# A Fourier transform and an MLP on one core: the opening reordered, and x folded by accumulating DMA

## The chip, the core and the metric

One core of a Trainium2 chip. The metric is the device time of one execution, in microseconds (us). A core has TensorE (PE; its weight loads are shown apart as PEld), VectorE (DVE), ScalarE (ACT), GpSimd (POOL) and SyncE (SP, which here only issues DMAs). Each takes its instructions in the order of the program. 16 DMA engines move what SyncE, ScalarE and GpSimd issue.

## The reference

Batch 8, sequence 3136, width 256. First the real part of a two-dimensional Fourier transform of each batch entry, then a layer norm and an MLP with a residual:

```
X = fft(fft(x, axis=1), axis=2).real                    # x: 8 x 3136 x 256
mu, var = mean(X, -1), mean((X - mu)**2, -1)
Xn = (X - mu) / sqrt(var + 1e-6) * g_ln
out = X + maximum(Xn @ w1, 0) @ w2                      # w1: 256 x 1024, w2: 1024 x 256, both float64
```

## The kernel before, in words

*The transform over the sequence.* 3136 = 56 x 56, so the kernel does it in two steps. The host gathers x's rows so that the rows n and 3136-n of 28 residues stand together: `xs` holds, per tile `i` of 7, two rows n and two rows 3136-n for each of 112 partitions, and `xz` the lone residue. `fold_zw` adds the row n and the mirrored row 3136-n (mirrored along the width), into `z` and `w`; `ends` does that for the columns 0 and 128 into `e0c`; for batch 0 VectorE does `fold_zw`, for the other batches GpSimd. Step 1 (`step1`, `step1_ends`) is a matmul with `tu` over those sums, in batch 0 in plain float32; in the other batches sums and differences (`fold_eo`, GpSimd) are split into a rounded high part (`fold_hi`, ScalarE) and a low part (`fold_lo`, GpSimd) and multiplied in three passes. ScalarE copies step 1's result to `s1`, `store1` writes it to `scratch` in HBM, `relayout` reads it back with other partitions into `s2`, and step 2 (`step2`) is a matmul of `s2` with the table `tab_s`. Its result is stored in chunks of 256 tokens: full (`ck`), high (`ckh`) and low part (`ckl`).

*The MLP.* w1 is multiplied by `g_ln` and the transform over the width on the chip (`transform_w1(k, i)` adds half `i` of column block `k`; `round_w1(k)` makes the high part, `rest_w1(k)` and `rest_w1_copy(k)` the low part). A tile `s` is 128 hidden columns for one chunk; eight make a chunk. `moe1_a(s)` is six matmuls into `ab`, ScalarE's copy `asb` and VectorE's two combinations `h`; `moe1_b(s)` makes `h_hi` (ScalarE) and `h_lo` (VectorE); `moe2(s)` is twelve matmuls into `acc`, three passes with w2's high and low part. `residual`, `finish` and `store_out` end a chunk. The main loop is

```
for s in range(6, last):
    moe1_b(s - 1); moe1_a(s)
    # then late[s], moe2(s - 3), after[s]
```

where `after` and `late` are lists, written out by tile number, of everything else: step 1 and step 2 of the next batches, the loads of the batch after that, residuals and stores. There are 392 tiles.

*The weights.* w1 and w2 arrive as 64-bit floats in four quarters each. `convert_m`, `convert_b` (VectorE) and `convert_z` (ScalarE) pick mantissa, exponent and sign apart; `finish_w1`/`finish_w2` multiply them; `split_w2` makes w2's high (ScalarE) and low part (VectorE; GpSimd for the last quarter). w1's raw quarters lie in four buffers, `w1p`, and w2's quarters are loaded into the same four when these are free; quarter `n` of w2 serves the tiles 2n and 2n+1 of a chunk.

*The order ahead of the main loop* is written out by hand, for TensorE, VectorE, ScalarE, GpSimd and SyncE's DMA queue alike. Before: x of batch 0 and w1, then w2's quarters 0 and 1 as soon as w1's first two buffers are free, the first relayout (groups 0 to 3, in two parts, the second behind the last two stores of step 1), the tables, w2's quarters 2 and 3, x of batch 1. TensorE transforms all of w1, then five empty matmuls (`warm_up`), `step2(0)`, `step2(1)`, and the tiles 0 to 5, with the conversion of w2's quarters 2 and 3 beside them.

Lines of the profile: L212 and L210 load x, L596 w1, L601 w2; L226, L230 and L231 `ends`; L246 and L247 `fold_zw`, L257 and L258 `fold_eo`, L263 `fold_hi`, L269 `fold_lo`; L280 to L288 `step1_ends`; L299 and L300 step 1 of batch 0, L305 of the others, L309 its copy, L315 `store1`; L323 `relayout`; L355 and L359 `step2`, L376 `ckh`, L378 `ck`, L380 `ckl`; L400, L405 to L407 `moe1_a`, L414 and L415 `moe1_b`, L450 `moe2`; L567 to L582 the conversions, L586 and L587 `split_w2`, L610 `finish_w1`, L620 `transform_w1`, L628 `round_w1`, L633 `rest_w1`, L638 `rest_w1_copy`, L642 `finish_w2`, L722 `warm_up`.

Of the kernel before, what the change touches and what calls it, by code (L numbers as in the profile page):

```python
# [25 lines left out]
ALU = mybir.AluOpType  # L26
# [145 lines left out]
def tile_kernel(ctx: ExitStack, tc: tile.TileContext, x, x0, w1, w2, tu, tab, ty, tw, out):  # L172
# [27 lines left out]
    xs = const.tile([XP, NU, 4, D], F32, name="xs")  # L200
    xz = const.tile([XP, D], F32, name="xz")
# [5 lines left out]

    def load_x(b, i):
        if i == NU:
            in_order(nc.sync.dma_start(xz, x0[b]))  # L210
        else:
            in_order(nc.sync.dma_start(xs[:, i], x[b, i]))  # L212

    e0c, s1, scratch, s2, zw, pieces = {}, {}, {}, {}, {}, {}

    def ends(b, p0=0, p1=NS, eng=nc.gpsimd):

        if p0 == 0:
            e0c[b] = work.tile([XP, NS, 2], F32, tag="e0c", name=f"e0c{b}")
        e = e0c[b]  # L220
        i0, i1 = (p0 + 1) // 2, p1 // 2
        for j0, j1 in ((i0, min(i1, 6)), (max(i0, 6), i1)):
            if j0 < j1:
                xp = xs[:, j0:j1, :, 0:129:128]
                s0 = first_slot(j0)
                eng.tensor_tensor(out=e[:, s0:s0 + 2 * (j1 - j0)].rearrange("p (i a) c -> p i a c", a=2),  # L226
                                  in0=xp[:, :, 0:2], in1=xp[:, :, 2:4], op=ALU.add)
        if p1 < NS:
            return
        eng.tensor_copy(e[:, LONE], xz[:, 0:129:128])  # L230
        eng.tensor_tensor(out=masked.rearrange("p (c s) -> p c s", c=4),  # L231
                          in0=e[:, None, :, 0].to_broadcast([XP, 4, NS]),
                          in1=tu_s[:, 3 * XP:3 * XP + 4, None].to_broadcast([XP, 4, NS]), op=ALU.mult)

    def fold_zw(b, i, eng):

        if i == NU:
            return
        if i > 3 and b == 0:
            t = weights.tile([128, HW], F32, tag="h_hi", name=f"zw{b}_{i}", bufs=4)  # L240
        else:
            t = work.tile([128, 2 * 256], F32, tag="zw", name=f"zw{b}_{i}", bufs=3)
        z, w = (t[:, 256 * h:256 * h + 256].rearrange("p (s d) -> p s d", s=2) for h in range(2))
        zw[b, i] = z, w
        a, c = xs[:, i, 0:2], xs[:, i, 2:4]
        eng.tensor_tensor(out=z, in0=a[:, :, 1:129], in1=c[:, :, 255:127:-1], op=ALU.add)  # L246
        eng.tensor_tensor(out=w, in0=a[:, :, 255:127:-1], in1=c[:, :, 1:129], op=ALU.add)  # L247
# [28 lines left out]
    def step1_ends(b, p0=0, p1=NS):  # L276
# [3 lines left out]
        nc.tensor.matmul(ps[:, 0], tu_p, e0c[b][:, p0:p1, 1], start=True, stop=True)  # L280
        nc.tensor.matmul(ps[:, 1], tu_h, e0c[b][:, p0:p1, 0], start=False, stop=True,
# [8 lines left out]
    def step1(b, i):  # L290
# [4 lines left out]
        if b == 0:  # L295
            z, w = zw.pop((b, i)) if n > 1 else (xz[:, None, 1:129], xz[:, None, 255:127:-1])
# [253 lines left out]
    def convert_e(key, wp):  # L550
# [3 lines left out]
        else:  # L554
            e = work.tile([128, 512], F32, tag="zw", name=f"e{key}", bufs=3)
# [43 lines left out]
    def load_w2(n):  # L599
        wp = w1p[n]  # L600
# [25 lines left out]
    def round_w1(k):  # L626
        for j in range(2):
            nc.scalar.copy(w1_cols(w1_hi, k, j), psw[k, j])  # L628
# [47 lines left out]
    for b in range(1, NB):  # L676
# [4 lines left out]
        add(need - 62 if b > 1 else ends_at - 7, ends, b)  # L681
        add(ends_at, step1_ends, b)
        for i, d in sorted(enumerate(at), key=lambda p: p[1]):
            d0, d = d, d - (b == 1)
            add(d - 7, fold_zw, b, i, nc.gpsimd)
            if b + 1 < NB:
                add(d - 5, load_x, b + 1, i)
# [37 lines left out]
    with tc.manual_schedule(engines={E.PE, E.Activation, E.DVE, E.Pool}):  # L725
        with tc.manual_schedule(engines={E.SP}):
# [46 lines left out]
            ends(0, 10, NS)  # L773
# [3 lines left out]
            fold_zw(0, 5, nc.vector)  # L777
# [6 lines left out]
            fold_zw(0, 6, nc.vector)  # L784
# [4 lines left out]
            relayout(0, 0, 4, LONE - 2)  # L789
# [13 lines left out]
            convert_b("w1_3")  # L803
            load_w2(3)
# [100 lines left out]
```

## Time and profile before

| | |
|---|---|
| median of 3 runs | 989.62 us (989.11 to 989.96) |
| profiled execution | 991.33 us, its span 989.5 us, TensorE clock 1.00 |
| TensorE busy | 977.6 us of the span, 99% |
| VectorE, ScalarE, GpSimd busy | 811.8, 538.4, 259.8 us |
| DMA | 94.69 MB, 96 GB/s in the mean; 343 GB/s in the first 23 us |
| TensorE busy from 0 to 23, 23 to 31, 31 to 36, 36 to 70 us | 19.98, 7.54, 3.02, 31.39 us |
| TensorE busy from 970 to the end (19.5 us) | 15.68 us |

A row of the busy times by stretch gives the stretch, its length, then for each engine its busy time and its count of instructions, the granted clock of TensorE, the share of the 16 DMA engines and GB/s. A row of the timeline has the start, the duration, engine, line, operation, the tile written and those read; in brackets how long the engine was idle before and what ended that. A group has busy time and mean duration. A DMA's issue is short; "to landing" is from its issue to the last byte.

### The profile page before, as it was taken

The numbers are of one execution on the slowest core, as the hardware profiler recorded it, in microseconds if no ns is written. First come the engines' busy times: TensorE is split into PE (matmuls) and PEld (weight loads), VectorE is DVE, ScalarE is ACT, GpSimd is POOL, SyncE is SP. The second block draws the span as 40 slices with busy tenths as digits, with TensorE's granted clock in tenths as the row PEclk, the third lists the DMA queues.
The fourth block names the chain that finished last, engine by engine and source line by source line (L and its number), as shares of the span: only waits on it lengthen the run. The fifth ranks groups of instructions, "written<-read, shape, count | busy, mean of one in ns | idle before, by whom it ended". The sixth has DMA issues, their size and how long they took to land.

```text
span 989.5 us, 22022 instructions
## 1 busy us (share of the span) xinstructions
PE 977.6 (99%) x8386; PEld 963.2 (97%) x8386; DVE 811.8 (82%) x2185; ACT 538.4 (54%) x1415; POOL 259.8 (26%) x312
## 2 busy tenths in 40 slices
PE   8899999999999999999999999999999999999998
PEld 6689999999999999999999999999999999999998
DVE  6788887888788788878878887888788888888887
ACT  3556555555555555565555555555655554454553
POOL 2046622334123421442223332233213500000000
PEclk9999999999999999999999999999999999999999
DMA  9933342224122232222322241222210112100101
GB/s 349 337 115 111 118 168 71 86 92 149 55 91 75 92 131 84 70 97 75 145 81 76 87 150 69 79 89 91 107 44 34 65 38 108 39 27 23 44 23 44
DMA packets 43673, 94.69 MB, mean 96 GB/s; under 512 B 3952, under 2 KB 20592, under 8 KB 42672
## 3 DMA queue, kind: packets, MB, share of 16 engines
q1 hardware_dynamic: 42352, 91.18, 25.9%
q8 instruction: 67, 1.10, 0.5%
q0 software_dynamic: 400, 1.31, 0.3%
q10 hardware_dynamic: 816, 0.79, 0.2%
q14 instruction: 38, 0.31, 0.1%
HBM read 51.58 MB, written 41.68 MB: 94 GB/s over the span
## 4 chain that ended last, share of the span: by engine, by line
PE 92%; DVE 4%; DMA 2%; ACT 1%; issue 0%; SPq 0%; ACTq 0%
PE acc L450 51%; PE ab L400 26%; PE ps L355 5%; PE psy L475 4%; PE ps L305 4%; DVE h_lo L415 1%; DMA xs<-x 1%; DMA scratch<-s 1%; DVE h L406 1%; DVE h L407 1%; PE ps L299 1%; ACT h_hi L414 0%; PE ps L300 0%; DMA s<-scratch 0%; PE ps L359 0%
## 5 line engine op out<-in xcount | busy, mean ns | idle before, releaser
L450 PE MATMUL acc<-w_hi,h_lo 128*128 128x256 f32 x1568 | 433.6, 277 | 0.2 <-DVE h_lo L415 0.2
L450 PE MATMUL acc<-w_lo,h_hi 128*128 128x256 f32 x1568 | 433.3, 276 | 0.0
L450 PE MATMUL acc<-w_hi,h_hi 128*128 128x256 f32 x1568 | 433.3, 276 | 0.0
L415 DVE SCALAR_TENSOR_TENSOR h_lo<-h,h_hi 128x512 fp32r<-128x512 f32 x392 | 286.0, 729 | 146.2 <-ACT h_hi L414 140.9
L414 ACT ACTIVATE h_hi<-h 128x512 fp32r<-128x512 f32 x392 | 250.1, 638 | 275.2 <-DVE h L407 272.4
L450 PEld LDWEIGHTS acc<-w_hi,h_lo 128*128 128x128 f32 x1568 | 294.5, 188 | 0.5 <-DVE h_lo L415 0.4
L450 PEld LDWEIGHTS acc<-w_lo,h_hi 128*128 128x128 f32 x1568 | 294.4, 188 | 0.0
L450 PEld LDWEIGHTS acc<-w_hi,h_hi 128*128 128x128 f32 x1568 | 294.4, 188 | 0.0
L400 PE MATMUL ab<-ckl,w_hi 128*128 128x256 f32 x768 | 219.0, 285 | 1.8 <-DVE h L407 1.6
L400 PE MATMUL ab<-ckh,w_lo 128*128 128x256 f32 x768 | 213.1, 277 | 0.8 <-ACT w_lo L638 0.5
L400 PE MATMUL ab<-ckh,w_hi 128*128 128x256 f32 x768 | 212.4, 277 | 0.0
L269 POOL TENSOR_TENSOR fl<-f,fh 128x512 fp32r<-128x512 f32 (+1 forms) x56 | 69.2, 1235 | 491.3 <-ACT fh L263 491.3
L406 DVE TENSOR_TENSOR h<-asb,ab 128x256 f32<-128x256 f32 x384 | 158.5, 413 | 1.5 <-ACT asb L405 1.4
L407 DVE TENSOR_TENSOR h<-asb,ab 128x256 f32<-128x256 f32 x384 | 158.4, 413 | 0.0
L400 PEld LDWEIGHTS ab<-ckl,w_hi 128*128 128x128 f32 x768 | 144.2, 188 | 3.2 <-issue 1.7
L400 PEld LDWEIGHTS ab<-ckh,w_lo 128*128 128x128 f32 x768 | 144.3, 188 | 1.2 <-ACT w_lo L638 0.7
L400 PEld LDWEIGHTS ab<-ckh,w_hi 128*128 128x128 f32 x768 | 144.3, 188 | 0.0
L405 ACT COPY asb<-ab 128x256 f32<-128x256 f32 x384 | 138.9, 362 | 4.7 <-PE ab L400 1.8
L309 ACT COPY s<-ps 128x508 f32<-128x508 f32 (+1 forms) x64 | 35.5, 556 | 72.6 <-PE ps L305 59.5
L376 ACT CAST ckh<-ps 128x448 fp32r<-128x448 f32 (+49 forms) x104 | 38.3, 371 | 50.2 <-PE ps L355 50.2
L355 PE MATMUL ps<-tab_s,s 120*128 120x112 f32 (+1 forms) x448 | 59.4, 275 | 2.0 <-DMA s<-scratch 2.0
L355 PEld LDWEIGHTS ps<-tab_s,s 120*128 120x128 f32 x448 | 54.6, 191 | 2.9 <-issue 2.4
(115 smaller groups left out, 1033.4 us busy)
## 6 DMA issues: line engine op xcount, KB each, us to landing
xs<-x SPq DMA_DIRECT2D x56, 512.0 KB, 3.6
out<-o SPq DMA_DIRECT2D x96, 256.0 KB, 2.0
s<-scratch SPq DMA_DIRECT2D x7, 1792.0 KB, 7.3
scratch<-s SPq DMA_DIRECT2D x42, 256.0 KB, 2.3
w1p_all<-w SPq DMA_DIRECT2D x8, 512.0 KB, 9.8
scratch<-s SPq DMA_DIRECT2D x7, 384.0 KB, 2.8
scratch<-s POOLq DMA_DIRECT2D x5, 256.0 KB, 6.5
xz<-x SPq DMA_DIRECT2D x8, 128.0 KB, 2.3
```

What stands on the lines that cost most here:

```text
L269: nc.gpsimd.tensor_tensor(out=lo, in0=f, in1=hi.bitcast(F32), op=ALU.subtract)
L305: nc.tensor.matmul(ps[:, a], (t1_hi, t1_lo)[ti], p[xi][:, a], start=(a == 0 and j == 0), stop=(j == 2), skip_group_check=True)
L355: nc.tensor.matmul(ps[:, h, k0 - base:k1 - base], s2[b][:KP, g, 128 * h:128 * h + 128], tab_s[:KP, h, k0:k1], start=(h == 0 and g == 2 * j ...
L376: nc.scalar.copy(hi, src)
L400: nc.tensor.matmul(pt, wt[wi][:, j, fs], ch[xi][:, j, :w], start=(n == 0), stop=(n == 2))
L405: nc.scalar.copy(asb[:, :w], pa)
L406: nc.vector.tensor_tensor(out=h[:, :w], in0=asb[:, :w], in1=pb, op=ALU.add)
L407: nc.vector.tensor_tensor(out=h[:, w:], in0=asb[:, :m], in1=pb[:, :m], op=ALU.subtract)
L414: nc.scalar.activation(h_hi, h, AF.Relu)
L415: nc.vector.scalar_tensor_tensor(out=h_lo, in0=h, scalar=0.0, in1=h_hi.bitcast(F32), op0=ALU.max, op1=ALU.subtract)
L450: nc.tensor.matmul(acc[c, i][:, side], hs[xi][:, h0:h0 + 128], ws[wi][:, f], start=(f == 0 and side == 0 and n == 0), stop=(f == 7 and n = ...
L475: nc.tensor.matmul(ps[:, j, :n], ck[:, j], ty_s[:, j, :n], start=(j == 0), stop=True, skip_group_check=True)
```

## The change

Four things, in one edit.

- x is laid out by the host as two halves, `[tile, partition, half, 2 rows, 256]`, the second already mirrored along the width, so that a fold is one addition of equal shapes. In batch 0 VectorE adds the second half onto the first in place (`fold_x`); the tile is loaded whole, into two runs of 2 KB per partition where there was one of 4 KB. From batch 1 on SyncE loads the first half (256 KB) and GpSimd issues a DMA that adds the second half onto it (`add_x`, `accum_op`), four tiles later in the main loop; batch 1's seven come ahead of it. `fold_zw`, `ends` and `e0c` go; `fold_eo`, `step1` and `step1_ends` read `xs` itself, and `edge_sums` is what is left of `ends`. In the main loop the loads of x move from tile d-5 to max(d-3, ends_at+1).
- w2's quarters 0 and 1 are loaded later: quarter 0 behind the issue of all stores, ahead of the first relayout, into w1's third buffer; quarter 1 behind the first relayout, into the fourth; 2 and 3 into the first and second.
- `transform_w1(1, 1)`, w1's second half of block 1, moves from ahead of `step2(0)` to behind the matmuls of tiles 0 and 1, and with it `round_w1(1)` and `rest_w1(1)`. Quarter 1 of w2 is converted in pieces around `step2` and tiles 0 to 2, in place of ahead of them; `moe2(0)` and `moe2(1)` come one tile earlier in TensorE's order.
- The empty matmuls ahead of `step2(0)` are two in place of five; the buffers `zw` are two in place of three.

The diff, cut to its core:

```diff
-    xs = const.tile([XP, NU, 4, D], F32, name="xs")
-    xz = const.tile([XP, D], F32, name="xz")
+    xs = const.tile([XP, 2, NS, D], F32, name="xs")
...
+    def x_slots(i, half=0):
+        s0 = first_slot(i)
+        return xs[:, half, s0:s0 + slots(i)]
     def load_x(b, i):
         if i == NU:
-            in_order(nc.sync.dma_start(xz, x0[b]))
+            in_order(nc.sync.dma_start(x_slots(i), x0[b][:, None]))
+        elif b == 0:
+            s0 = first_slot(i)
+            nc.sync.dma_start(xs[:, :, s0:s0 + 2], x[b, i])
         else:
-            in_order(nc.sync.dma_start(xs[:, i], x[b, i]))
+            in_order(nc.sync.dma_start(x_slots(i), x[b, i][:, 0]))
+    def fold_x(i):
+        nc.vector.tensor_tensor(out=x_slots(i), in0=x_slots(i), in1=x_slots(i, 1), op=ALU.add)
+    def add_x(b, i):
+        nc.gpsimd.dma_start(x_slots(i), x[b, i][:, 1], accum_op=ALU.add)
+    def edge_sums():
+        nc.gpsimd.tensor_tensor(out=masked.rearrange("p (c s) -> p c s", c=4),
+                                in0=xs[:, 0, None, :, 0].to_broadcast([XP, 4, NS]),
+                                in1=tu_s[:, 3 * XP:3 * XP + 4, None].to_broadcast([XP, 4, NS]),
+                                op=ALU.mult)
+    def halves(i):
+        x = x_slots(i)
+        return x[:, :, 1:129], x[:, :, 255:127:-1]
...
     def load_w2(n):
-        wp = w1p[n]
+        wp = w1p[(n + 2) % 4]
...
-    def round_w1(k):
-        for j in range(2):
+    def round_w1(k, js=(0, 1)):
+        for j in js:
...
-        add(need - 62 if b > 1 else ends_at - 7, ends, b)
+        add(ends_at - (2 if b > 1 else 7), edge_sums)
...
-            add(d - 7, fold_zw, b, i, nc.gpsimd)
             if b + 1 < NB:
-                add(d - 5, load_x, b + 1, i)
+                t = max(d - 3, ends_at + 1)
+                add(t, load_x, b + 1, i)
+                if i < NU:
+                    add(t + 4, add_x, b + 1, i)
...
             convert_b("w1_0")
-            load_w2(0)
...
             convert_b("w1_1")
-            load_w2(1)
-            relayout(0, 0, 4, 0, LONE - 2)
-            nc.sync.dma_start(tab_s[:, :, :gb[4]], tab[:, :, :gb[4]])
...
-            relayout(0, 0, 4, LONE - 2)
...
             finish_w1(2)
-            load_w2(2)
-            nc.sync.dma_start(tab_s[:, :, gb[4]:gb[8]], tab[:, :, gb[4]:gb[8]])
-            relayout(0, 4, 8)
-            relayout(0, 8, NG)
+            load_w2(0)
+            relayout(0, 0, 4, 0, LONE - 2)
+            nc.sync.dma_start(tab_s[:, :, :gb[4]], tab[:, :, :gb[4]])
+            relayout(0, 0, 4, LONE - 2)
             nc.scalar.copy(minus, tw_all[:, 512:])
             transform_w1(0, 0)
             transform_w1(0, 1)
             convert_m("w1_3", w1p[3])
             convert_b("w1_3")
+            load_w2(1)
+            load_w2(2)
+            nc.sync.dma_start(tab_s[:, :, gb[4]:gb[8]], tab[:, :, gb[4]:gb[8]])
+            relayout(0, 4, 8)
+            relayout(0, 8, NG)
             load_w2(3)
...
             finish_w1(3)
+            round_w1(0, (0,))
             convert_z("w2_0", w2p[0])
-            round_w1(0)
+            round_w1(0, (1,))
             transform_w1(1, 0)
             rest_w1(0)
-            transform_w1(1, 1)
             convert_m("w2_0", w2p[0])
             convert_b("w2_0")
-            w2f.append(finish_w2(0))
-            convert_z("w2_1", w2p[1])
+            split_w2(0, finish_w2(0))
+            rest_w1_copy(0)
             convert_m("w2_1", w2p[1])
-            convert_b("w2_1")
-            w2f.append(finish_w2(1))
-            split_w2(0, w2f.pop(0))
-            rest_w1_copy(0)
-            round_w1(1)
-            split_w2(1, w2f.pop(0))
-            warm_up(5, warm_h)
+            warm_up(2, warm_h)
             step2(0, "m")
             step2(0, "hl")
+            convert_z("w2_1", w2p[1])
             step2(1, "m")
             step2(1, "hl", 0)
+            convert_b("w2_1")
             moe1_a(0, ((1, 0), (0, 0), (0, 1)))
+            moe1_a(1, ((1, 0), (0, 0), (0, 1)))
             step2(0, "f")
-            moe1_a(1, ((1, 0), (0, 0), (0, 1)))
+            transform_w1(1, 1)
+            moe1_b(0)
+            round_w1(1)
+            f = finish_w2(1)
+            moe1_b(1)
+            moe1_a(2)
+            split_w2(1, f)
+            moe2(0)
             rest_w1(1)
-            moe1_b(0)
-            moe1_a(2)
-            moe1_b(1)
             moe1_b(2)
             moe1_a(3)
             rest_w1_copy(1)
             step2(1, "f")
             convert_a("w2_2", w2p[2])
             step2(1, "hl", 1)
-            moe2(0)
+            moe2(1)
             moe1_b(3)
             moe1_a(4)
             convert_b("w2_2")
             f = finish_w2(2)
+            for i in range(NU):
+                add_x(1, i)
             nc.gpsimd.tensor_scalar(out=neg, in0=ty_s[:, 1, 129:130], scalar1=2.0, scalar2=-1.0,
                                     op0=ALU.mult, op1=ALU.add)
-            moe2(1)
             step2(2, "m")
...
+    x = np.stack([x[..., :2, :], x[..., 2:, -np.arange(D) % D]], 3)
```

In batch 0 `fold_x(i)` stands where `fold_zw(0, i, nc.vector)` stood, and one `edge_sums()` ahead of the last `step1_ends` in place of three `ends`.

More of the change, by code (lines that the diff above doesn't have):

```diff
@@ L206, in tile_kernel @@
     single = const.tile([128, 2, 2 * NB], F32, name="single")
+    def x_slots(i, half=0):
+        s0 = first_slot(i)
+        return xs[:, half, s0:s0 + slots(i)]
     def load_x(b, i):
         if i == NU:
-            in_order(nc.sync.dma_start(xz, x0[b]))
-        else:
-            in_order(nc.sync.dma_start(xs[:, i], x[b, i]))
[L214 to L247, printed above, removed]
+            in_order(nc.sync.dma_start(x_slots(i), x0[b][:, None]))
+        elif b == 0:
+            s0 = first_slot(i)
+            nc.sync.dma_start(xs[:, :, s0:s0 + 2], x[b, i])
+        else:
+            in_order(nc.sync.dma_start(x_slots(i), x[b, i][:, 0]))
@@ new lines, in fold_x @@
+    def fold_x(i):
+        nc.vector.tensor_tensor(out=x_slots(i), in0=x_slots(i), in1=x_slots(i, 1), op=ALU.add)
+    def add_x(b, i):
+        nc.gpsimd.dma_start(x_slots(i), x[b, i][:, 1], accum_op=ALU.add)
+    scratch, s1, s2, pieces = {}, {}, {}, {}
+    def edge_sums():
[3 more added lines that the diff above has]
+                                op=ALU.mult)
@@ L254, in fold_eo @@
         n = slots(i)
-        z, w = zw.pop((b, i)) if n > 1 else (xz[:, None, 1:129], xz[:, None, 255:127:-1])
+        z, w = halves(i)
         f = work.tile([128, 2, 2, 128], F32, tag="fold", name=f"f{b}_{i}")[:, :n]
@@ L279, in step1_ends @@
         ps = psum.tile([128, 3, n], F32, tag="y" if b else "fft", name=f"pse{p0}_{b}")
-        nc.tensor.matmul(ps[:, 0], tu_p, e0c[b][:, p0:p1, 1], start=True, stop=True)
-        nc.tensor.matmul(ps[:, 1], tu_h, e0c[b][:, p0:p1, 0], start=False, stop=True,
+        nc.tensor.matmul(ps[:, 0], tu_p, xs[:, 0, p0:p1, 128], start=True, stop=True)
+        nc.tensor.matmul(ps[:, 1], tu_h, xs[:, 0, p0:p1, 0], start=False, stop=True,
                          skip_group_check=True)
@@ L295, in step1 @@
         if b == 0:
-            z, w = zw.pop((b, i)) if n > 1 else (xz[:, None, 1:129], xz[:, None, 255:127:-1])
+            z, w = halves(i)
             for h, t in ((0, tu_p), (1, tu_n)):
@@ L554, in convert_e @@
         else:
-            e = work.tile([128, 512], F32, tag="zw", name=f"e{key}", bufs=3)
+            e = work.tile([128, 512], F32, tag="zw", name=f"e{key}", bufs=2)
         conv[key] = wp.bitcast(I32).rearrange("p (n two) -> p n two", two=2)[:, :, 1], e
@@ L747, in tile_kernel @@
             nc.gpsimd.memset(zmu, 0.0)
-            ends(0, 0, 6)
-            fold_zw(0, 0, nc.vector)
+            fold_x(0)
             step1(0, 0)
             nc.vector.tensor_scalar_mul(g_s, tu_s[:, 3 * XP + 4 + R1 + 1:], 2.0 ** -20)
-            fold_zw(0, 1, nc.vector)
+            fold_x(1)
             convert_z("w1_0", w1p[0])
@@ L757, in tile_kernel @@
             convert_m("w1_0", w1p[0])
-            fold_zw(0, 2, nc.vector)
+            fold_x(2)
             step1(0, 2)
             convert_b("w1_0")
-            load_w2(0)
             step1_ends(0, 0, 6)
-            ends(0, 6, 10)
             for i in range(3):
                 store1(0, i, nc.gpsimd)
-            fold_zw(0, 3, nc.vector)
+            fold_x(3)
             step1(0, 3)
             convert_z("w1_1", w1p[1])
-            fold_zw(0, 4, nc.vector)
+            fold_x(4)
             step1(0, 4)
@@ L772, in tile_kernel @@
             step1_ends(0, 6, 10)
-            ends(0, 10, NS)
             store1(0, 3, nc.gpsimd)
@@ L776, in tile_kernel @@
             convert_m("w1_1", w1p[1])
-            fold_zw(0, 5, nc.vector)
+            fold_x(5)
             step1(0, 5)
@@ L780, in tile_kernel @@
             convert_b("w1_1")
-            load_w2(1)
-            relayout(0, 0, 4, 0, LONE - 2)
-            nc.sync.dma_start(tab_s[:, :, :gb[4]], tab[:, :, :gb[4]])
-            fold_zw(0, 6, nc.vector)
+            fold_x(6)
+            edge_sums()
             step1_ends(0, 10, NS)
```

## The prediction

> **What bounds the kernel now.** I read the page's first part, the busy time by stretches, TensorE's list of waits, the chain that ended last, and then the queues. First the page and the stretches (us; busy time and, in brackets, instructions of each engine; clock, DMA share, GB/s):
>
> ```profile
> PE 977.6 (99%) x8386; PEld 963.2 (97%) x8386; DVE 811.8 (82%) x2185; ACT 538.4 (54%) x1415; POOL 259.8 (26%) x312
> ...
> L415 DVE SCALAR_TENSOR_TENSOR h_lo<-h,h_hi 128x512 fp32r<-128x512 f32 x392 | 286.0, 729 | 146.2 <-ACT h_hi L414 140.9
> ```
>
> ```profile
> 23.00:31.00 8.00, 7.54 (x19) 3.52 (x20) 7.20 (x14) 4.00 (x9) 0.00 (x0) 1.00 0.89 305
> 31.00:36.00 5.00, 3.02 (x20) 2.05 (x18) 2.84 (x5) 2.60 (x6) 0.00 (x0) 1.00 0.90 255
> 36.00:70.00 34.00, 31.39 (x252) 29.64 (x251) 29.83 (x72) 18.97 (x49) 9.10 (x14) 1.00 0.56 217
> 70.00:970.00 900.00, 900.00 (x7892) 898.20 (x7891) 742.94 (x2022) 499.36 (x1322) 244.09 (x282) 1.00 0.24 83
> ```
>
> From 70 to 970 us TensorE is busy for 900 of 900 us at clock 1.00, so a shorter wait of another engine there buys nothing; behind 970 lies only the last chunk. The change can gain only ahead of 70 us, and lose anywhere. The two views of that head, TensorE's longest wait (in total, times, longest) and the chain (start, duration):
>
> ```profile
> PE ps L355 <- DMA s<-scratch: 2.0, 1, 2.0
> ```
>
> ```profile
> 3.09 8.43 DMA xs<-x
> ...
> 23.20 7.19 DMA scratch<-s
> 30.41 3.56 DMA s<-scratch
> ...
> 36.96 1.01 PE ab L400 x6
> ...
> 44.87 0.55 DVE ckl L380
> ...
> 66.52 0.94 PE ab L400 x6
> ```
>
> So: batch 0's third x tile lands (11.5), its transform runs on TensorE, the last store into scratch takes 7.19 us under full queues, the relayout 3.56, then `step2(0)` starts. In the chain's pieces from 44.87 to 66.5 VectorE is nearly everything: converting w2's second half beside the MLP tiles makes it the bound there. I call A the first `ab` matmul of tile 0: 36.96 before.
>
> **The change, part by part.**
>
> *1. w2's quarters 0 and 1 behind the stores.* SyncE's queue, and landings in the page's list of DMA issues (KB each, us to landing) and in the answer for the w2 load issued at 30.84:
>
> ```profile
> 14.15 4.99 SPq L601 DMA_DIRECT2D w1p_all<-w  x2
> 26.84 0.34 SPq L323 DMA_DIRECT2D s<-scratch  x1
> ...
> 30.84 0.39 SPq L601 DMA_DIRECT2D w1p_all<-w  x1
> ```
>
> ```profile
> xs<-x SPq DMA_DIRECT2D x56, 512.0 KB, 3.6
> ...
> scratch<-s SPq DMA_DIRECT2D x42, 256.0 KB, 2.3
> ...
> scratch<-s POOLq DMA_DIRECT2D x5, 256.0 KB, 6.5
> ...
> scratch<-s ACTq DMA_DIRECT2D x1, 256.0 KB, 7.2
> ```
>
> ```profile
> DMA to landing us min/median/max: 5.0/5.0/5.0
> ```
>
> The second relayout goes out at 30.41 (the chain), when the last store (issued 23.20) has landed. Quiet, such a store lands in 2.3 us (25.5); loaded it takes 7.2. After the change quarter 0 shares w1's third buffer and waits for its conversion, so it is issued near 22 and still competes; quarter 1 is gone from ahead of the store. 512 KB at the 400 or so GB/s of full queues is 1.3 us. Bounds: 0 (the slowest DMA engine is not relieved) to -4.9 (quiet). I take -1.3, nearest to the loaded row because quarter 0, the other stores, the first relayout and the table stay: second relayout at 29.1, landed at 32.7 with 3.56, all of `step2` as before, A at 35.65.
>
> ```profile
> 36.36 0.80 DVE L380 TENSOR_TENSOR ckl<-ps,ckh 128x446 fp32r<-128x446 f32 x2 [2.24 <-ACT ckh L376]
> ```
>
> Quarter 1 now goes out right behind that relayout, where quarter 2 took 5.0 us before; a quiet 512 KB load takes 3.6. So it lands between 33.1 and 34.5. VectorE has `convert_m(w2_1)` (L567 and L569 in the groups below, 0.43+0.69 = 1.1 us) ahead of `step2(0)`'s `ckl`, and tile 0 needs both `ckl` pieces (the row above, 0.8 us) some 0.3 after A, behind four `ab` matmuls: A = landing + 1.6 = 34.7 to 36.1. That is a new wait, about level with the relayout's. I take A = 35.65: **-1.3** (range -4.0 to +0.5). TensorE itself would be free by 29.8 (two warm-ups behind 29.17, where `transform_w1(1, 1)` began before; the three warm-ups that go stood in the wait and count for nothing).
>
> *2. The second half of w1's second transform, and quarter 1's conversion, behind the first tiles.* Rows of the timeline, then the groups that are moved (busy us, mean ns):
>
> ```profile
> 29.17 1.88 PE L620 MATMUL psw<-gw,tw_all 128*128 128x512 f32 x4
> ...
> 38.40 0.42 DVE L406 TENSOR_TENSOR h<-asb,ab 128x256 f32<-128x256 f32 x1 [1.24 <-ACT asb L405]
> 38.50 0.63 PE L633 MATMUL psw<-w_hi,minus 128*128 128x512 f32 x2
> ...
> 41.40 1.47 DVE L415 SCALAR_TENSOR_TENSOR h_lo<-h,h_hi 128x512 fp32r<-128x512 f32 x2
> ...
> 46.33 0.41 DVE L407 TENSOR_TENSOR h<-asb,ab 128x256 f32<-128x256 f32 x1
> ```
>
> ```profile
> L582 DVE SCALAR_TENSOR_TENSOR ew<-w1p_all,ew 128x512 int32<-128x512 int32 x8 | 5.5, 692 | 0.3
> L569 DVE SCALAR_TENSOR_TENSOR fw<-w1p_all,mw 128x512 f32<-128x512 uint32 x8 | 5.5, 692 | 0.3
> ...
> L567 DVE TENSOR_SCALAR mw<-w1p_all 128x512 int32<-128x512 int32 x8 | 3.5, 434 | 2.6 <-DMA w1p_all<-w 2.5
> ...
> L580 DVE TENSOR_SCALAR ew<-ew 128x512 int32<-128x512 int32 x8 | 3.4, 420 | 0.2
> ...
> L642 DVE SCALAR_TENSOR_TENSOR fw<-fw,ew 128x512 f32<-128x512 f32 x4 | 2.8, 692 | 0.1
> L587 DVE TENSOR_TENSOR w_lo<-fw,w_hi 128x512 fp32r<-128x512 f32 x3 | 2.1, 688 | 0.3 <-ACT w_hi L586 0.2
> ```
>
> ```profile
> L628 ACT CAST w_hi<-psw 128x512 fp32r<-128x512 f32 x4 | 2.2, 596 | 0.0
> ```
>
> TensorE's 4 matmuls (1.7 us issued) lay in the wait for the relayout; that cover is gone, and they now come after tile 1. Part of them fills pauses that TensorE has in the first tiles. VectorE gets `convert_b` (0.42+0.69 = 1.1), the product (0.69) and the low part (0.69) of quarter 1 among its tiles. The first fits the 1.24 us that it idled ahead of tile 0's `h`; 1.4 us do not. ScalarE gets the quarter's exponent step and high part (each of the L628 row's shape, 0.6) and `round_w1(1)`, two of that row, 1.2. `round_w1(1)` waits for the transform, which starts when two tiles are through (38.50, A+1.54) and ends 1.88 later, and runs until A+4.6, and `h_hi` of tile 1 behind it until A+5.2, so VectorE's `h_lo` of tile 1, at A+4.44 before (41.40), starts at A+5.2 though VectorE was ready at A+4.6: 0.6 of waiting. Behind `rest_w1_copy(1)` ScalarE is late once more for the second chunk's `ckh`: 0.3. Tile 4's `h`, which ended at A+9.7 before (second half at 46.33), ends 1.4+0.6+0.3 = 2.3 later against A. VectorE being the bound until 66.5, this stays: **+2.3**. Bounds: +1.4 (ScalarE hides everything) to +3.
>
> *3. x folded by layout.* Batch 0: one 128x512 addition per tile in place of two 128x256; at 0.69 (the L587 row, the same shape) against two halves it saves little, where the chain follows DMA and TensorE: 0. x's runs in SBUF are halved to 2 KB, which w2's already are; a stretch of x alone against one of w2 and store runs:
>
> ```profile
> 46.00:48.00 2.00, 2.00 (x19) 2.00 (x19) 1.93 (x6) 0.63 (x1) 0.00 (x0) 1.00 1.04 424
> 22.50:23.50 1.00, 0.09 (x2) 0.04 (x1) 1.00 (x2) 0.58 (x1) 0.00 (x0) 1.00 1.05 410
> ```
>
> 3% of the 8.43 us to the third tile is 0.25, half of it absorbed by the queues behind: **+0.1** (0 to +0.3). [...] `edge_sums` replaces `ends`; it sits behind two stores on POOL, at most 0.2 late. From batch 1 on, GpSimd loses `fold_zw`; its additions had held up VectorE, visible as long `h_lo` beside its own additions (0.73 in the mean):
>
> ```profile
> 64.52 1.20 DVE L415 SCALAR_TENSOR_TENSOR h_lo<-h,h_hi 128x512 fp32r<-128x512 f32 x1 [0.70 <-ACT h_hi L414]
> ```
>
> I count **-0.4** (0 to -0.8) before 66 us, nothing after 70 us.
>
> *4. Accumulating DMAs from POOL's queue: 7 ahead of the main loop, 42 in it.* No row has one. POOL's nearest, its five stores, and the work behind the first seven:
>
> ```profile
> L315 POOL DMA_DIRECT2D scratch<-s x5 | 3.8, 764 | 0.4 <-ACT s L286 0.4
> ```
>
> ```profile
> 56.02 1.28 POOL L587 TENSOR_TENSOR w_lo<-fw,w_hi 128x512 fp32r<-128x512 f32 x1 [12.50 <-ACT w_hi L586]
> ...
> 57.59 0.28 PE L450 MATMUL acc<-w_lo,h_hi 128*128 128x256 f32 x1
> ```
>
> POOL waits for each plain half before it issues the accumulation. If the first half lands at 46 (half the bytes, similar queue), seven issues at 0.76 end near 51.5, ahead of w2's last low part (56.02), which tile 6's second product needs at 57.59. In the loop the last accumulation of a batch has 4 tiles until `edge_sums` and 2 more until TensorE's `step1_ends` needs it; 392 tiles in 950 us are 2.4 us each, so 14.5 us against 6.5 to land. On SyncE's queue x's plain halves move from five to at most three tiles ahead of a transform, in front of the stores as before, half as large, and a batch (48 tiles) ahead of their use. What hides all this is the distance to TensorE's need; were it gone, TensorE would lose each wait in full. Cost **0**; bounds 0 to +7 (issues of 2 us or more, below).
>
> Sum: -1.3+2.3+0.1-0.4 = +0.7. The low side of the first term is wider than the high one, so I take +0.5. The profiled execution took 991.33 (span 989.5, 1.8 around it), 1.7 above the median of the runs shown, 989.62; the difference goes onto the median: 990.1.
>
> **The rivals.**
> *The DMA queues clear at once (0.11).* With the stores ahead, the last lands in a quiet 2.3 us, and TensorE, ready at 29.8, and quarter 1 set A at 33. For it: 1 MB leaves the stretch. Against: quarter 0 and the table stay in it. -4.0+2.3-0.4 = -2.1: 987.5, faster.
> *A wait for quarter 1 replaces the wait for the relayout (0.13).* The last store is not relieved, quarter 1 lands at 35.9 as quarter 2 did, VectorE holds `ckl` behind `convert_m`, A stays near 37.2: +0.2+2.3-0.2 = +2.3, 991.9. It decides once the landing passes 35. For it: 5.0 us at just that place.
> *POOL's accumulations hold up w2's last low part (0.12), slower.* An issue of over 1.4 us ends the seven after 56; at 2.0 they end at 60, the low part at 61.3, TensorE needs it at 58.1: +3.2 on top of 0.5, 993.3. Against: 0.76 of the plain stores, beside a busy VectorE. [...]
>
> **How the numbers follow.** The forecast has 0.64, and with its bounds reaches from 988.6 to 991.6. 0.2% (2.0 us) is about what a measurement can tell from no change. Faster: the first rival and little else, 0.12. Slower: the third, and over half of the second, 0.20. Same: 0.68. The range takes in the second rival and the forecast, 988.0 to 992.5.
>
> **What would show it.** Right: `ps` matmuls start near 32.8 in place of 34.10, with a wait of a DMA or of `ckl` ahead of A near 35.7; four L620-type matmuls after tile 1; `h_lo` of tile 1 waiting for ScalarE; TensorE without pauses from about 70. Wrong: a last store landed by 27, `ckl` late behind a DMA wait of the second w2 conversion by over a microsecond, POOL issues above 1.4 us, or any TensorE pause between 70 and 970.

## The result and the profile after

The changed kernel takes 998.44 us in the median (994.45 to 1001.09, 6 executions) against 989.97 (989.11 to 992.76, 6) of the kernel before beside it: ratio 1.0084, 95% interval 1.0066 to 1.0103. It is slower by 8.5 us and lies outside the range of 988.0 to 992.5. The profiled execution took 998.25 us, with a span of 996.3. One execution of experiment 7 below, its profiled one, took 1098.96 us at a mean clock of 0.839; it is left out there, and no time is read from its profile.

The page's busy times, and the granted clock in 40 slices (the second digit, 7, is new):

```profile
PE 980.6 (98%) x8382; PEld 965.1 (97%) x8383; DVE 814.7 (82%) x2178; ACT 541.1 (54%) x1415; POOL 211.2 (21%) x237
...
PEclk9799999999999999999999999999999999999999
```

The same stretches as before (stretch, length, busy time of PE, PEld, DVE, ACT and POOL, clock, DMA share, GB/s):

```profile
23.00:31.00 8.00, 6.80 (x17) 2.69 (x16) 5.83 (x11) 3.19 (x6) 0.00 (x0) 1.00 0.99 299
31.00:36.00 5.00, 2.82 (x11) 2.55 (x12) 1.81 (x3) 1.59 (x3) 0.00 (x0) 0.63 1.05 344
36.00:70.00 34.00, 31.09 (x220) 28.31 (x220) 27.53 (x62) 19.79 (x49) 12.10 (x14) 0.90 0.68 188
70.00:970.00 900.00, 897.80 (x7877) 895.43 (x7877) 744.78 (x2016) 499.95 (x1316) 194.08 (x212) 1.00 0.29 84
```

Between 36 and 70 us TensorE is as busy as before (31.09 us against 31.39) and gets through 220 matmuls in place of 252: it is not waiting, it is slow, at a mean clock of 0.90. From 70 to 970 it is busy for 897.80 us of 900 where it was busy for all of them. So there are two losses, and the start of the output stores prices them. The first rows are of the changed kernel, the others of the kernel before (first and last store of each):

```profile
72.42 0.34 SPq L520 DMA_DIRECT2D out<-o  x1
...
993.32 0.33 SPq L531 DMA_DIRECT2D out<-o  x1
```

```profile
67.97 0.34 SPq L531 DMA_DIRECT2D out<-o  x1
...
986.53 0.33 SPq L542 DMA_DIRECT2D out<-o  x1
```

The opening, up to the first store, is longer by 72.42 - 67.97 = 4.45 us. From first to last store it is 920.90 us, in the kernel before 918.56: the main loop is longer by 2.3. How far one profile can be trusted here: the same loop took 918.92 and 917.52 in experiments 4 and 9, which leave it as it was.

**The opening.** TensorE's longest waits, and the chain up to w1's moved transform:

```profile
PE ab L389 <- DVE h L396: 4.0, 9, 0.8
PE ps L344 <- DMA s<-scratch: 3.0, 1, 3.0
...
PE pse L273 <- POOL masked L229: 0.8, 1, 0.8
```

```profile
23.93 4.58 DMA scratch<-s
28.59 4.46 DMA s<-scratch
34.95 2.84 PE ps L344 x12
38.08 2.93 PE ab L389 x12
41.01 2.52 PE psw L609 x4
```

The DMA part went the way that was predicted: the last store lands in 4.58 us in place of 7.19, the second relayout is issued at 28.59 in place of 30.41 and landed at 33.05, and `step2(0)` starts 0.9 us earlier than before. But A, which was to be 35.65, is 38.08: twelve `ab` matmuls take 2.93 us where six took 1.01. The clock's record in this trace rises at 4.96 us, falls at 32.27, rises at 42.51 and falls at 994.82, behind the last matmul: 27.31, 10.24 and 952.32 us, 8, 3 and 279 times 3.41 (3.413). In the kernel before it has 983.04 us from the rise at 5.75 to the fall behind the last matmul, 288 times that. With the trace cut in stretches of this length, counted from the clock's first rise:

```profile
28.85:32.27 3.42, 1.17 (x4) 0.30 (x3) 2.67 (x5) 1.60 (x4) 0.00 (x0) 1.00 1.01 227
32.27:35.68 3.41, 2.50 (x10) 2.23 (x10) 1.21 (x3) 0.34 (x1) 0.00 (x0) 0.50 1.06 380
35.68:39.09 3.41, 3.10 (x14) 2.84 (x14) 1.61 (x4) 1.32 (x3) 0.00 (x0) 0.50 1.01 390
39.09:42.51 3.42, 3.42 (x12) 2.39 (x11) 1.80 (x6) 1.77 (x5) 0.00 (x0) 0.50 1.04 394
42.51:45.92 3.41, 3.41 (x24) 2.84 (x23) 2.46 (x5) 2.49 (x5) 0.95 (x1) 1.00 1.06 401
```

In the first of these TensorE is busy for 1.17 us of 3.42, since it waits for the relayout from 30.20 to 33.18; at its end the clock fell to 0.50 and stayed there for 10.24 us, three such stretches.

**The main loop.** The chain after 75 us has three pieces of a kind that the chain of before did not have:

```profile
122.68 2.50 DVE h_lo L404
...
352.04 2.72 DVE h_lo L404
...
701.31 2.23 DVE h_lo L404
```

An `h_lo` takes 0.7 us otherwise. The timeline about the first of them, GpSimd and then VectorE (start, duration):

```profile
121.07 1.29 POOL L258 TENSOR_TENSOR fl<-f,fh 128x512 fp32r<-128x512 f32 x1 [2.74 <-ACT fh L252]
122.32 0.86 POOL L224 DMA_DIRECT2D xs<-x  x1
122.92 1.02 POOL L246 TENSOR_TENSOR f<-xs 128x256 f32<-128x256 f32 x1
123.61 1.01 POOL L247 TENSOR_TENSOR f<-xs 128x256 f32<-128x256 f32 x1
124.29 1.17 POOL L224 DMA_DIRECT2D xs<-x  x1
```

```profile
122.60 2.58 DVE L404 SCALAR_TENSOR_TENSOR h_lo<-h,h_hi 128x512 fp32r<-128x512 f32 x1
125.11 0.41 DVE L395 TENSOR_TENSOR h<-asb,ab 128x256 f32<-128x256 f32 x1
```

The accumulating DMA's issue (L224) stands directly ahead of `fold_eo`'s two additions, which are ready, and a second such issue behind them. VectorE's instruction starts within the first issue and ends within the last. Behind 75 us there are ten VectorE instructions of 1.6 to 2.72 us (before: none over 1.36), and five pauses of TensorE, 2.2 us together. Of the DMAs themselves:

```profile
L224 POOL DMA_DIRECT2D xs<-x x49 | 43.5, 952 | 153.8 <-DMA xs<-x 86.3
```

```profile
xs<-x POOLq DMA_DIRECT2D x49, 256.0 KB, 4.2
```

### The profile page after: what moved, and what is told of

It is laid out like the page before. It is cut to its first block, busy times and chain, and to the rows that moved or that the text cites. A ratio compares the mean times of both kernels' runs of the same rounds, so it can differ in the third digit from the quotient of the medians.

```text
span 996.3 us, 21972 instructions
## 1 busy us (share of the span) xinstructions
PE 980.6 (98%) x8382; PEld 965.1 (97%) x8383; DVE 814.7 (82%) x2178; ACT 541.1 (54%) x1415; POOL 211.2 (21%) x237
## 4 chain that ended last, share of the span: by engine, by line
PE 88%; DVE 7%; DMA 2%; ACT 2%; issue 1%; SPq 0%; POOL 0%; POOLq 0%; ACTq 0%
PE acc L439 49%; PE ab L389 25%; PE ps L344 5%; PE psy L464 4%; PE ps L294 3%; DVE h_lo L404 2%; DVE h L395 1%; DVE h L396 1%; DMA w1p_all<-w 1%; DMA xs<-x 1%; ACT h_hi L403 1%; DVE st L486 0%; DMA scratch<-s 0%; DMA s<-scratch 0%; PE ps L348 0%
## 5 line engine op out<-in xcount | busy, mean ns | idle before, releaser
L224 POOL DMA_DIRECT2D xs<-x x49 | 43.5, 952 | 153.8 <-DMA xs<-x 86.3
```

Source lines behind the costliest of these rows:

```text
L224: nc.gpsimd.dma_start(x_slots(i), x[b, i][:, 1], accum_op=ALU.add)
```

## The experiments

Eleven kernels, each against the kernel before on its chip. "A" is the first `ab` matmul of tile 0, "loop" the time from first to last output store, "half clock" how long the clock stood at 0.50 in the profiled execution between the start and 75 us (all us).

| kernel | median (range, count) | ratio to before, 95% | A | first store | loop | half clock |
|---|---|---|---|---|---|---|
| before, with the change | 989.97 (989.11 to 992.76, 6) | | 36.96 | 67.97 | 918.56 | 0 |
| the change | 998.44 (994.45 to 1001.09, 6) | 1.0084, 1.0066 to 1.0103 | 38.08 | 72.42 | 920.90 | 10.24 |
| 1: 14 warm-ups | 995.05 (993.88 to 996.34, 7) | 1.0034, 1.0022 to 1.0047 | 35.67 | 68.44 | 921.92 | 0 |
| 2: x folded by GpSimd | 1001.39 (1000.81 to 1001.89, 5) | 1.0098, 1.0083 to 1.0113 | 38.43 | 77.13 | 918.98 | 10.24 + 6.83 |
| 3: 1 and 2 | 1000.48 (998.13 to 1003.96, 6) | 1.0092, 1.0072 to 1.0113 | 36.12 | 73.84 | 921.39 | 6.83 |
| 4: before, 2 warm-ups | 992.25 (989.72 to 994.87, 12) | 1.0005, 0.9992 to 1.0017 | 38.35 | 71.17 | 918.92 | 10.24 |
| 5: opening alone | 991.64 (990.59 to 994.7, 12) | 1.0004, 0.9992 to 1.0016 | 36.12 | 68.87 | 917.76 | 0 |
| 6: x alone | 994.33 (990.89 to 997.16, 12) | 1.0030, 1.0016 to 1.0044 | 36.17 | 67.37 | 921.13 | 0 |
| 7: 1, DMAs moved | 989.96 (988.95 to 990.73, 11) | 0.9981, 0.9970 to 0.9992 | | | | |
| 8: 7, transform early | 989.65 (988.45 to 990.76, 12) | 0.9979, 0.9967 to 0.9992 | 35.98 | 67.50 | 916.66 | 0 |
| 9: before, 12 warm-ups | 991.05 (990.12 to 992.58, 12) | 0.9987, 0.9977 to 0.9998 | 37.00 | 68.00 | 917.52 | 0 |
| 10: x alone, DMAs moved | 989.31 (988.96 to 990.17, 12) | 0.9968, 0.9955 to 0.9980 | 37.28 | 67.94 | 916.86 | 0 |
| 11: 5 warm-ups | 996.40 (992.35 to 999.29, 12) | 1.0034, 1.0018 to 1.0050 | 36.72 | 70.98 | 920.56 | 6.83 |

The kernel before had medians of 990.92 beside 1 to 4, 991.5 beside 5 to 8 and 992.93 beside 9 to 11, 82 executions in all. Experiment 4 shows why they differ: in some executions of that kernel the clock falls too (6 of 18, 19 of 35 and 16 of 29). Those whose mean clock was 0.999 or more, "at full clock" from here on, have medians of 990.69, 990.45 and 991.06.

**1. The wait filled with empty matmuls.**

```diff
-            warm_up(2, warm_h)
+            warm_up(14, warm_h)
```

> The changed kernel with 14 empty matmuls ahead of step2(0) in place of 2; they fill the 3 us in which TensorE waited for the relayout. Clock theory: the changed kernel lost its time in the opening because TensorE's clock fell to one half from 32.3 to 42.5 us after that wait; then the clock stays at 1.00, tile 0's first ab matmul comes near 36 in place of 38.1, the first store of an output near 68.5 in place of 72.4, and the time falls by 3.5 to 4.5 us, to about 994. Rival (the conversion and transform moved among the first tiles hold VectorE and ScalarE): the clock stays up but the first output store moves by less than 1.5 us and the time stays above 996.5.

The clock stays at 1.00, A is at 35.67, and the first store comes 4.0 us earlier than in the changed kernel; the medians are 3.4 apart. Of the 4.0, 0.5 is that the second relayout landed at 32.57 in this profile and at 33.05 in that one. The loop keeps its loss: 921.92, with eleven VectorE instructions of up to 2.57 us. So the halved clock is a loss of its own of about 3.5 us, and what is left has nothing to do with it.

**2. No accumulating DMA: x loaded whole, GpSimd adds.**

```diff
-            in_order(nc.sync.dma_start(x_slots(i), x[b, i][:, 0]))
+            s0 = first_slot(i)
+            in_order(nc.sync.dma_start(xs[:, :, s0:s0 + 2], x[b, i]))
...
-        nc.gpsimd.dma_start(x_slots(i), x[b, i][:, 1], accum_op=ALU.add)
+        nc.gpsimd.tensor_tensor(out=x_slots(i), in0=x_slots(i), in1=x_slots(i, 1), op=ALU.add)
```

> The changed kernel, but from batch 1 on SyncE loads both halves of x and GpSimd adds the second onto the first with an instruction, where the accumulating DMA stood; no DMA is issued by GpSimd behind the opening's five stores. Theory of the port: VectorE's instructions of 2 to 2.7 us in the main loop (normal 0.7) come from GpSimd issuing an accumulating DMA beside its own additions; then no VectorE instruction there takes over 1.5 us, TensorE's pauses between 70 and 970 us (2.2 us in the profile) go, and the time falls by about 2 us, to 996.4, with the opening as it was. Rival (the pauses in the main loop belong to the late opening or to x's distance): VectorE's long instructions and the pauses stay, the time stays within 0.7 us of 998.4.

The loop is 918.98, the kernel before's within 0.4 us, but not for the reason expected: eleven `h_lo` still take 1.53 to 1.82 us, beside GpSimd's additions, and TensorE still pauses twice, for 0.7 us together. The total missed by far: the seven additions of batch 1 now stand beside the hand-written opening, where VectorE is the bound (busy for 3.38 of the 3.41 us from 52.57), and one row each of GpSimd and VectorE shows what they do to an instruction of 0.69 us:

```profile
49.59 7.93 POOL L225 TENSOR_TENSOR xs<-xs 128x512 f32<-128x512 f32 x5
```

```profile
49.94 1.67 DVE L559 SCALAR_TENSOR_TENSOR fw<-w1p_all,mw 128x512 f32<-128x512 uint32 x1
```

TensorE pauses for 2.21 and 2.91 us, and the clock falls a second time, for 6.83 us. The first store is 4.7 us later than the changed kernel's. "The port" in this expectation and the next was a guess of mine at what VectorE and GpSimd share; no run shows one.

**3. Both edits.**

> Both edits together: 14 empty matmuls, and x added by GpSimd's instruction. If the clock and the port are the two causes and add up: 6 us less than the changed kernel, about 992, which is 2 us above the kernel before, the share of VectorE's and ScalarE's moved work in the prediction (2.3). If the moved work costs nothing after all: 989 to 990. If the clock has nothing to do with it: 996.

It missed for the same reason: A is early, but a pause of 4.96 us ahead of 56.97 halves the clock again, and the first store is at 73.84. Its loop, without an accumulating DMA, is 921.39, nearly as long as that of 1; TensorE's pauses there are 0.9 us, and the rest is not explained. So 2 and 3 do not show that the loop's loss leaves with the accumulating DMAs; 5 to 8 and 10 have to.

**4. The kernel before with fewer warm-ups.**

```diff
-            warm_up(5, warm_h)
+            warm_up(2, warm_h)
```

> The kernel before with 2 empty matmuls in place of 5, nothing else: TensorE's wait ahead of step2(0) grows from 1.98 to 2.6 us. If a wait of that length is enough for the clock to fall, half clock for about 10 us and 3 to 5 us more, 993 to 995. If the clock falls only at waits of 3 us and more, the time of the kernel before, 990, with a granted clock of 1.00 throughout.

Its wait is 2.29 us. In the profiled execution (994.87) the clock fell for 10.24 us and the first store came at 71.17; yet the median moved little, because the clock fell in some executions and not in others, here and in the kernel before alike: 8 of 12 here had a mean clock of 0.998 or less (one stretch of 3.41 us at 0.50 lowers it by 0.0017), 6 of 18 there.

**5 and 6. The change in two.** The first has x as before and the new opening order with 14 warm-ups; the second has x's layout and accumulating DMAs, the old order and 5 warm-ups.

> The kernel before with the changed order of the opening alone (w2's loads, the transform, the conversions), 14 empty matmuls so that the clock stays up, and x as before: folded by fold_zw and ends, no accumulating DMA. If the accumulating DMAs cost the main loop what the changed kernel shows there (first to last output store 920.9 to 921.9 us against 918.6 before), its main loop is as before, 918.6 within 0.3; the first store is at 68.5 to 69, because A comes 1.3 us earlier and VectorE's and ScalarE's moved work takes 1.8 to 2.3 back; the time is 0.5 to 1 us above the kernel before. If the main loop stays at 921 the DMAs are not its cause.

> x's new layout, fold and accumulating DMAs alone, with the kernel before's order of w2's loads, of the transform and of the conversions, and its 5 empty matmuls. If the DMAs are the main loop's cause: first store near 68.0 as before, main loop 920.9 to 922, the time 2.5 to 3.5 us above the kernel before. If the moved opening work is the cause of everything: as the kernel before.

The opening order alone has no long VectorE instruction, no pause of TensorE after 75 us and a loop of 917.76; its first store is 0.9 us later than before. In the medians that is a tie, but 19 of the 35 executions beside it had lost their clock: at full clock it takes 991.53 against 990.45, so this order costs 1.1 us. x's part alone has an opening that is 0.6 us shorter in its profile, and the whole loss of the loop: 921.13, ten VectorE instructions of up to 2.75 us; at full clock 993.23 against 990.45.

**7 and 8. The accumulating DMAs put elsewhere in GpSimd's order.** In 7, `add_x` goes to slots behind the next piece's `fold_eo` and ahead of a `fold_lo`, which waits for ScalarE; 8 also takes w1's last transform back ahead of the tiles, with 8 warm-ups.

```diff
-                if i < NU:
-                    add(t + 4, add_x, b + 1, i)
...
+        if b + 1 < NB:
+            adds = [need - d for d in (49, 42, 38, 29, 25, 18, 10)] if b > 1 else [19, 19, 24, 26, 29, 31, 35]
+            for i, t in enumerate(adds):
+                add(t, add_x, b + 1, i)
```

> e1_warm14 with each accumulating DMA of the main loop moved in GpSimd's order: behind the next piece's additions (fold_eo) and ahead of a subtraction that waits for ScalarE, so that no addition that is ready stands right behind a DMA. If VectorE is held for as long as GpSimd's DMA and the additions right behind it run on without a break: no VectorE instruction over 1.5 us, the main loop within 0.7 us of 918.6, 2 to 3 us less than e1_warm14, about 0.5 to 1 above the kernel before. If the DMA alone holds VectorE, whatever stands behind it: long instructions of 1.5 us and more stay and the time is within 0.7 us of e1_warm14.

> e7_add_order with transform_w1(1, 1), round_w1(1) and rest_w1(1) ahead of the tiles again, in TensorE's wait for the relayout, and 8 empty matmuls behind them. By the prediction's step 2, 0.9 us of the moved work's price were ScalarE's waits for that transform and some of TensorE's 1.7 us: the first store comes 0.9 to 1.7 us earlier than in e7_add_order, near 67, and the time is 0.5 to 1 us below the kernel before. If VectorE's share alone sets the price, no change against e7_add_order.

Both have a lower median than either kernel, 7 by more than expected; against the kernel before at full clock they gain 0.5 and 0.8 us. The early transform is worth 0.3 in the medians (8 against 7). In 8 the loop is 916.66, without a pause and without a VectorE instruction over 1.37 us. The same 49 DMAs now cost nothing: the place in GpSimd's order was the price, not the bytes and not the issue. The moves shifted each DMA by some tiles as well, but the traces point at the order: of the changed kernel's 42 issues in the main loop 18 have an addition right behind them, and each of its ten long VectorE instructions runs beside the additions of such a run; in 8 and 10 none of the 42 has.

**9. The kernel before with 12 warm-ups.**

> The kernel before, with 12 warm-ups ahead of step2(0) in place of 5. Theory (the kernel before has the same weakness: its 1.98 us wait of TensorE ahead of step2(0) is enough to lose the clock in some of its executions, at 2 to 4 us each): seven more warm-ups of 0.2 us leave a wait of about 0.6 us, every execution keeps clock 1.00, none of them lies above 991.5, the median is 989.3 to 990.3 and at most 0.2% under that of the kernel before. Rival (the executions of 992 to 994 come from something else, such as the chip's power): they stay as frequent, and the median equals that of the kernel before within 0.3 us, with executions above 992.

All 12 executions ran at clock 1.00 (0.999 or more), where 16 of the 29 of the kernel before beside them did not. The median of 991.05 is that of the kernel before at full clock, 991.06. The theory on the clock holds; "none above 991.5" does not, since three executions at full clock took 991.80 to 992.58. Those have another cause, which stays open.

**10. x alone, DMAs moved, 12 warm-ups.**

> x's part alone (layout, accumulating DMA, the kernel before's opening order), with add_x moved in GpSimd's order behind fold_eo and ahead of a fold_lo, and 12 warm-ups. Theory (the accumulating DMAs cost only through their place in GpSimd's order, and x's part is worth nothing by itself otherwise): no VectorE instruction above 1.5 us and no TensorE pause between 75 and 970, first output store near 67.4 as in the run of x's part alone, main loop 916.7 to 918.6, total 988.6 to 990.5; against the best version so far (989.65) the opening order is then worth nothing measurable. Rival (the early opening order is what makes the best version faster): 990.5 or more, level with the kernel before.

989.31, the best of all, with all 12 executions between 988.96 and 990.17. GpSimd's order now, and the stretch of the main loop:

```profile
104.08 0.74 POOL L246 TENSOR_TENSOR f<-xs 128x256 f32<-128x256 f32 x1
104.79 1.25 POOL L247 TENSOR_TENSOR f<-xs 128x256 f32<-128x256 f32 x1
105.97 0.87 POOL L224 DMA_DIRECT2D xs<-x  x1
111.65 1.28 POOL L258 TENSOR_TENSOR fl<-f,fh 128x512 fp32r<-128x512 f32 x1 [4.80 <-ACT fh L252]
```

```profile
70.00:970.00 900.00, 899.94 (x7904) 897.84 (x7903) 732.76 (x2027) 501.20 (x1323) 201.93 (x212) 1.00 0.28 83
```

Behind the issue GpSimd is idle for 4.80 us, and VectorE is busy for 732.76 us, 10 less than in the kernel before. Against 9 on the same chip x's part is worth 1.7 us in the medians; the opening order adds nothing to it that can be measured (8 against 10, on two chips).

**11. The changed kernel with 5 warm-ups.**

> The changed kernel with 5 warm-ups in place of 2, so that only the moved transform (1.88 us of matmuls) is missing ahead of the wait. Theory (length of the wait decides): the wait of TensorE ahead of step2(0) is 2.98 - 3 x 0.2 = 2.4 us, between the 1.98 and 2.98 of the two kernels; the clock is lost in more executions than in the kernel before and in fewer than in the changed kernel; median 995.5 to 998, single executions at 994 to 995 with clock 1.00 and near 998 without. Rival (any wait above 2 us loses it always, or the transform's matmuls alone keep the clock): all executions at 997.5 to 999, as the changed kernel; or, if the three warm-ups were the whole of it, all at 994 to 995.5.

The wait was 1.85 us, shorter than expected, and still the clock fell for 6.83 us in the profiled execution; it fell in 6 of the 12. The median of 996.40 lies between the changed kernel's and experiment 1's. Single executions are not told apart as cleanly as expected: 992.35 to 996.67 at full clock, 996.33 to 999.29 without. So neither the transform nor the three warm-ups are the whole of it: the length of the wait decides, and where it lies.

**What the length is measured against.** Stretches of 3.41 us counted from the clock's first rise, as above, around TensorE's wait: experiment 11, then 6, then 4.

```profile
30.79:34.21 3.42, 1.57 (x11) 1.20 (x10) 1.25 (x3) 1.59 (x3) 0.00 (x0) 1.00 0.97 303
34.21:37.62 3.41, 3.11 (x15) 2.84 (x15) 2.42 (x6) 1.32 (x3) 0.00 (x0) 0.50 1.05 364
```

```profile
30.21:33.62 3.41, 1.89 (x9) 0.79 (x9) 3.26 (x6) 2.57 (x6) 0.00 (x0) 1.00 0.97 258
33.62:37.04 3.42, 3.12 (x25) 2.77 (x24) 0.97 (x3) 0.74 (x2) 0.00 (x0) 1.00 1.03 353
```

```profile
30.02:33.43 3.41, 1.08 (x3) 0.21 (x3) 2.92 (x5) 2.07 (x4) 0.00 (x0) 1.00 0.87 257
33.43:36.85 3.42, 3.40 (x14) 3.12 (x15) 0.00 (x0) 0.47 (x1) 0.00 (x0) 0.50 1.03 392
```

And the kernel before, where the wait is cut in two by a border:

```profile
29.64:33.06 3.42, 2.48 (x9) 0.82 (x7) 3.29 (x6) 3.33 (x7) 0.00 (x0) 1.00 0.84 245
33.06:36.47 3.41, 2.37 (x18) 2.23 (x18) 0.95 (x3) 0.87 (x2) 0.00 (x0) 1.00 0.97 279
```

In these traces the clock fell at the end of a stretch in which TensorE was busy for 1.57 us or less, and did not where it was busy for 1.89 or more. All six falls ahead of 75 us follow a stretch in which TensorE was idle for 1.85 to 2.97 us, and no stretch with 1.52 us or less was followed by one: the limit lies between 1.52 and 1.85, and I estimate it at half of 3.41, 1.71. The fall behind TensorE's last matmul, in each of these traces, fits as well (it follows a stretch with 2.06 us idle or more, and none with 1.41 or less). The kernel before waits 1.98 us, over that limit, and kept its clock in this profile, where a border cuts the wait into 0.94 and 1.04. An estimate from these numbers: if borders fall anywhere, 1.98 us puts more than 1.71 into one stretch in (3.41 - 1.98 + 2 x 0.27)/3.41 = 58% of the executions; of its 82 beside the experiments, 41 had a mean clock of 0.998 or less. By the same estimate the changed kernel's 2.98 us does it in 87%: all six of its executions read 0.998 or less, five of them 0.997 or less. That estimate does not cover experiment 6, where 7 of 12 read 0.997 or 0.998 with a profiled wait of 1.47; how long those executions waited isn't known.

## Why the prediction was wrong

Two steps failed, the warm-ups in step 1 and the 0 of step 4, and none of the rivals had either loss.

**Step 1, the stores: about right, the warm-ups wrong.** Second relayout at 28.59 (predicted 29.1), landed at 33.05 (32.7), and with the wait filled A is at 35.67 (35.65). That agreement is in part luck. The store gained 2.6 us where 1.3 was predicted, but was issued 0.7 later, and the relayout took 4.46 where 3.56 was predicted. With the clock up, A lies between 36.17 and 37.28 in the four profiles with the old order and between 35.67 and 36.12 in the four with the new one: 0.9 in the mean, not 1.3. Quarter 1 landed at 34.2 in experiment 1 (33.1 to 34.5 was forecast), and tile 0's `ckl`, behind its conversion, was ready 0.4 us after A: level with the relayout's wait, as forecast. In the changed kernel itself A is 38.08. The failed words are those on the warm-ups: "the three warm-ups that go stood in the wait and count for nothing". They, and the 1.88 us of `transform_w1(1, 1)` that left the same wait, kept TensorE busy; without them a wait of 1.98 us became one of 2.98, and the clock was halved for 10.24 us. That costs 3.5 us: the first store stands 39.37 us behind the second relayout's landing, in experiment 1 35.87. I had looked for the wait that ends last and held the time inside it to be free.

**Steps 2 and 3, the moved transform and x's layout: about right.** They were to give +2.3, +0.1 and -0.4, so +1.9 behind A, ahead of which the +0.1 lies. In experiment 1 the first store stands 32.77 us behind A, in the kernel before 31.01: +1.8. Alone, the order gives +1.7 (experiment 5) and x's part +0.2 and -0.4 (6 and 10). I had put 0.9 us down to ScalarE's waits for the moved transform; experiment 8, with the transform back, has its first store 0.9 us ahead of that of 1, but the medians of 7 and 8 are only 0.3 apart. `edge_sums` is 0.8 us late once, predicted 0.2 at most, and the last store is issued at 23.65 to 24.60 in the eight profiles with x's part against 22.51 to 23.22 in the four without: ahead of A, x's part costs more than the +0.1. The opening that is 0.6 us shorter in experiment 6 is not shorter in 10 (67.94 against 67.97).

**Step 4, the accumulating DMAs at 0: wrong.** They cost 2.3 us of the loop in the changed kernel and 3.4 with 1, each read from one profile. I had asked how long GpSimd's issues take (0.87 us in the median, near the 0.76 of the stores), whether the bytes come in time (4.2 us), and whether VectorE holds GpSimd up. None of that hurt. Three of the seven issues in the opening took over the 1.4 us that I had named as a sign, up to 1.93 (the bound of +7, for issues of 2 us or more, is shown by no run), but they overlap: from the second on one began every 0.6 to 0.9 us, the last at 49.46, and the rival with w2's last low part did not occur. The loss went the other way, GpSimd's issue and the additions behind it holding up VectorE, at a step that had no term for VectorE. The 0 was right for the place that experiments 8 and 10 give them. I also counted nothing after 70 us for `fold_zw`'s departure; VectorE's 10 us less in experiment 10 suggest that it frees something there, if little for TensorE.

The sum for the changed kernel from the traces: +4.0 (the clock's 3.5 and the 0.5 of the relayout's landing) +0.47 (the rest of the opening, 68.44 - 67.97) +2.3 (loop) = +6.8, against +6.9 between the two profiled executions (998.25 - 991.33). The medians are 8.5 apart; of the 1.6 us between, 1.4 is that the profiled execution of the kernel before lay above its median (991.33 against 989.97) and 0.2 that the changed kernel's lay below.

Open: what in the hardware holds VectorE. The trace of the changed kernel narrows it. Beside an issue and no addition `h_lo` takes at most 0.69 us (16 times), so an issue alone does not hold it. Beside additions alone, in the kernel before, it takes up to 1.35. Only an issue with additions right behind it gives 2 us and more. The traces show which instruction is held: `h_lo`, which reads the tiles `h` and `h_hi`, and not `h`, which reads TensorE's result `ab` and never takes over 0.42 us. They show the length too: 2.58 us, across two GpSimd additions of 1.0 us each. What holds it, and why an issue ahead lengthens the hold, is not shown.

## What to carry to other kernels

A wait of TensorE was not free space here: with 2 empty matmuls in it the clock stood at 0.50 for 10.24 us, with 14 it stayed at 1.00. Where a change takes work out of such a wait, put empty matmuls in its place and measure the clock again; in these traces no stretch of 3.41 us with 1.52 us idle or less was followed by a fall. Look at the clock stretch by stretch ahead of the loop, and price a fall: here it cost about a third of the 7 to 10 us that it lasted, 3.5 us for 10.24 in the changed kernel, 2.4 for 6.83 in experiment 11 (its first store stands 38.24 us behind the relayout's landing, that of 1 35.87). Where GpSimd issues DMAs among its own additions, place the issue behind them and ahead of something that waits; a small change of order was worth 5 us here (experiments 1 and 7: 995.05 and 989.96).

## What the hardware showed that I had not expected

- In these traces the clock fell by how much of a stretch of 3.41 us TensorE was idle (1.85 us did it, 1.52 did not), not by the length of a wait alone, and the border of the stretches near the wait lay at another time in each profile (at 32.27 in the changed kernel, 33.06 in the one before, 33.43, 33.62 and 34.21 in experiments 4, 6 and 11). By the estimate above, that may be why the same kernel ran with and without the fall: a mean clock of 0.998 or less in 41 of 82 executions of the kernel before.
- In the six falls profiled it stayed at 0.50 for two stretches (6.83 us) or three (10.24). In each case the last of them was one without any pause of TensorE; one with a pause of 0.02 us (experiment 4, 33.43 to 36.85) did not end it.
- An accumulating DMA of 256 KB landed in 4.2 us where a plain load of that size took 3.3, and its issue on GpSimd took 0.87 us (medians of 49 each).
- GpSimd's 128x512 additions ran at 1.59 us each (7.93 for five, experiment 2), and VectorE's instruction beside them went from 0.69 to 1.67 us, more than the 128x256 ones of the kernel before did (1.35 at most).
